# Threshold attention and a SoLU feed-forward: keys turned by VectorE's block transposes instead of TensorE, keys and values loaded in longer runs

## The chip, the cores and the metric

The kernel runs on one core of a Trainium2 chip. Its time is the device time of one execution in microseconds (us); lower is better. The core has five engines that run at once, each through its own list of instructions in order: PE (TensorE, matrix products, with PEld its weight loads), DVE (VectorE), ACT (ScalarE), POOL (GpSimd) and SP (SyncE, which here only issues transfers). Transfers run on 16 DMA engines. SBUF is the memory that all engines work on, PSUM the one that PE writes its products to.

## The reference

There are 8 batches of 8 heads, 576 positions and 64 dimensions, all float32. Per head:

```python
scores = scale * np.matmul(q, k.transpose(0, 1, 3, 2))
thresh = np.max(scores, axis=-1, keepdims=True) - tau
scores = np.where(scores >= thresh, scores, -1000000000.0)
attn = np.exp(scores - np.max(scores, axis=-1, keepdims=True))
attn = attn / (np.sum(attn, axis=-1, keepdims=True) + 1e-09)
out = np.matmul(attn, v)
```

The heads are put side by side (4608 tokens of 512), and each token goes through a feed-forward block: `h = x @ w_in` (1024 wide), `h * softmax(h)`, a layer norm with gain `g_ln`, and `@ w_out`.

## The kernel before, in words

**Pairs and slots.** Two heads make a pair, four pairs (`NP`) a batch, 32 pairs in all; pair i is (b, hp). A pair's q and k are turned so that the 64 dimensions lie on partitions, the first head on rows 0 to 63 and the second on rows 64 to 127 (`ROWS`). A *slot* is a unit of attention, 18 for each batch (`PER`), 144 in all: 128 queries of one pair against its 576 keys (kinds 0 and 1), or, in the last two slots of a batch (kind 2), the 64 last rows ("ends") of two pairs at a time. The main loop (L789) makes one *round* for each slot and hands out each engine's instructions in a fixed, hand-written order. No planner changes it.

**One round.** PE first turns what a later pair needs (`turn`, L281: products with an identity matrix, into the spare columns of the scores' PSUM), then computes the scores (L417). DVE takes the row maximum (L439), ACT the ramp that puts what lies under the threshold out of play (L454) and the exponential (L463), POOL scales by the sum (L473), and DVE turns the weights in blocks of 32 x 32 (L485, tile T). After every second slot SP moves T to wT by four transfers (L496), so that the keys lie on partitions. Three rounds after the slot, PE multiplies wT by v (L521, tile pv). The scores' PSUM has one buffer for each head, so the next scores wait for the ramp and for the copies of turned data (`keep` functions) that were made from it.

**Feed-forward between.** Beside the attention, each round takes half of one of the feed-forward's two products: rounds in which half of the first product runs (h_ps, L577 or L567) are called *hidden rounds* here, those with half of the second (o_ps, L681) *output rounds*. A tile of tokens takes four rounds, in a cycle of two hidden and two output rounds. In the steady stage the products pv are taken in hidden rounds alone. Between the two products lie the softmax and norm (L592 to L648), a swap of parts by four transfers V<-u (L659), and a block transpose (L669, uT).

**Turning q and k.** For pairs from batch 1 on, a list `preps` (L727) says from which round on a pair is turned: k in two items (3 and 1 units), the ends (1 unit) and q (4 units), with room for 7 units in a round. A unit is four calls of `matmul` on 64 x 64 tiles. So k and the ends go in one round and q in the next. What PE has turned is copied out of PSUM, one row half by ACT and the other by DVE: L345 for k, L365 for the ends of k, L361 for the ends of q, L320 and L324 for q. Pairs 0 to 3 are turned through own buffers (tp) at the start.

**Loads.** q and k come four heads at a time (L129), rows 0 to 511 as runs of four positions (1024 bytes), and the 64 end rows in runs of 256 bytes (L140). v comes for four heads in three such parts (L159) and two parts of end rows (L164); both row halves hold all keys in an order of their own (`m ^ 4 * u` in L522). `load_at` (L741) says after which round each load is issued; SP issues them all in order, between the moves of wT, the swaps and the stores of the output.

**Buffers.** `loads` has two buffers for each of q, k and ends and three for v; `heads` has seven for each of qT, kT and qe (a pair's turned q, k and end queries).

Of the kernel before, what the change touches and what calls it, by code (L numbers as in the profile page):

```python
# [8 lines left out]
F32 = mybir.dt.float32  # L9
# [7 lines left out]
P = 128  # L17
# [3 lines left out]
def kernel(  # L21
# [27 lines left out]
    nc = tc.nc  # L49
    B, H, S, D = q.shape  # L50
    DM, DFF = w_in.shape
    SM = 512
    ST = S - SM
    NP = H // 2
    NPAIR = B * NP
    NC = DFF // P
# [3 lines left out]
    ROWS = (slice(0, 64), slice(64, P))  # L60

    const = ctx.enter_context(tc.tile_pool(name="const", bufs=1))
    loads = ctx.enter_context(tc.tile_pool(name="loads", bufs=2))
    heads = ctx.enter_context(tc.tile_pool(name="heads", bufs=7))
    work = ctx.enter_context(tc.tile_pool(name="work", bufs=2))
# [11 lines left out]
    zero = const.tile([P, 1], F32, name="zero")  # L77
    ntau = const.tile([P, 1], F32, name="ntau")
    scl = const.tile([P, 1], F32, name="scl")
    g_rows = const.tile([NC, P], F32, name="g_rows")  # L80
    gs = const.tile([P, NC], F32, name="gs")
    lims = [const.tile([P, 1], F32, name=f"lim{x}") for x in range(2)]

# [5 lines left out]
    NK = S // 64  # L89

    halves = {}
    ends = {}
    pairs = {}
    units = {}
# [25 lines left out]
    def load_one(b, hf, nm, queue=None):  # L120
        d = halves.setdefault((b, hf), {})
        hs = slice(4 * hf, 4 * hf + 4)
        src, rows = {"q": (q, ROWS[0]), "k": (k, ROWS[1])}[nm]
        d[nm] = loads.tile([P, 4, 4, D], F32, tag=nm, name=nm)

        parts = [slice(0, 2), slice(2, 4)] if b == 0 and hf == 0 else [slice(0, 4)]
        for x, part in enumerate(parts):
            queue = nc.scalar if nm == "k" and x + 1 < len(parts) else nc.sync
            queue.dma_start(  # L129
                out=d[nm][:, part].rearrange("p h t d -> p h (t d)"),  # L130
                in_=src[b, hs, 0:SM, :][part].rearrange("h (p t) d -> p h (t d)", t=4),
            )
            if hf == 0 and x == 0:
                if b not in ends:
                    ends[b] = loads.tile([P, H, D], F32, tag="ends", name="ends")
                load_ends(b, nm, slice(0, 2) if len(parts) > 1 else slice(0, H), queue)
# [11 lines left out]
    def load_v(b, hf, parts=(0, 1, 2)):  # L148
        d = halves.setdefault((b, hf), {})
        hs = slice(4 * hf, 4 * hf + 4)  # L150

        if 0 in parts:
            d["v"] = loads.tile([P, 4, NK, D], F32, tag="v", bufs=3, name="v")
        rest = v[b, hs, 0:SM, :].rearrange("h (p t) d -> p h (t d)", t=4)
        for part, to, rows, of in (
            (0, 0, slice(0, P), slice(0, P)), (1, 4, ROWS[0], ROWS[1]), (1, 4, ROWS[1], ROWS[0])
        ):
            if part in parts:
                nc.sync.dma_start(  # L159
                    out=d["v"][rows, :, to : to + 4].rearrange("p h t d -> p h (t d)"),  # L160
                    in_=rest[of],
                )
        for rows in ROWS if 2 in parts else ():
            nc.sync.dma_start(  # L164
                out=d["v"][rows, :, NK - 1], in_=v[b, hs, SM:S, :].rearrange("h p d -> p h d")
            )

    def constants():
# [109 lines left out]

    SPARE = 7

    def turn(spare, x, lhsT_of):  # L281

        o = spare["base"] + 64 * x
        to = slice(o, o + 64)
        for r in range(2):
            for y in range(2):
                nc.tensor.matmul(
                    out=spare[r][ROWS[y], to], lhsT=lhsT_of(r, y), rhs=ident[ROWS[r], ROWS[r]],
                    start=True, stop=True,
                )  # L290
# [9 lines left out]
    def pair(i):  # L300
        if i not in pairs:
            pairs[i] = dict(
                qT=heads.tile([P, SM], F32, tag="qT", name="qT"),
                kT=heads.tile([P, S], F32, tag="kT", name="kT"),
                qe=heads.tile([P, ST], F32, tag="qe", name="qe"),
            )
        return pairs[i]
# [23 lines left out]
    def k_parts(i):  # L331

        return pair(i)["kT"].rearrange("p (c m k) -> p m c k", c=2, m=NK)

    def k_item(i, ts=slice(0, 4)):
        src, h0 = source(i)
        to = k_parts(i)
        n = ts.stop - ts.start

        def make(spare, x):  # L340
            for t in range(n):
                turn(spare, x + t, lambda r, y: src["k"][ROWS[r], h0 + y, ts.start + t])

        def keep(spare, x, r):
            (nc.vector.tensor_copy if r and not spare.get("eased") else nc.scalar.copy)(  # L345
                out=to[:, 4 * r + ts.start : 4 * r + ts.stop],
                in_=seen(spare, r, x, n).rearrange("p t (k c) -> p t c k", c=2),
            )

        return n, make, keep  # L350

    def e_item(i):
        src, h0 = source(i)
        last = k_parts(i)[:, NK - 1]

        def make(spare, x):
            turn(spare, x, lambda r, y: ends[i // NP][ROWS[r], 2 * (i % NP) + y])

        def keep(spare, x, r):
            if r == 0:  # L360
                nc.scalar.activation(  # L361
                    out=pair(i)["qe"], in_=seen(spare, 0, x, 1)[:, 0], func=AF.Copy, scale=scl
                )
            else:
                (nc.scalar.copy if spare.get("eased") else nc.vector.tensor_copy)(  # L365
                    out=last, in_=seen(spare, 1, x, 1)[:, 0].rearrange("p (k c) -> p c k", c=2)
                )

        return 1, make, keep
# [130 lines left out]
    def attend_steps(key):  # L500
        b, kind, hp = key
        unit = units[key]
        wT = unit["wT"]
        unit["y"] = take("pv")
        _, y = unit["y"]
        y = y.rearrange("p (u n) -> p u n", u=2)

        for e in range(2) if kind == 2 else [None]:
            for m in range(NK):
                for u in range(2):  # L510
                    d, h0 = source(b * NP + (hp if e is None else e + 2 * u))
                    for h in range(2):
                        if e is None:
                            to = y[ROWS[h], u, 0:P].rearrange("p (r g x) -> p g r x", r=2, g=2)
                            rhs = wT[ROWS[u], :, m, :, h]
                        else:
                            to = y[ROWS[h], u, 64 * e : 64 * e + 64].rearrange(
                                "p (g x) -> p g x", g=2
                            )
                            rhs = wT[ROWS[u], :, m, e, h]  # L520
                        nc.tensor.matmul(  # L521
                            out=to, lhsT=d["v"][ROWS[u], h0 + h, m ^ 4 * u if m < 8 else m],  # L522
                            rhs=rhs,
                            start=m == 0, stop=m == NK - 1,
                        )
                        yield
# [188 lines left out]
    PER = NS // B  # L715
# [11 lines left out]
    preps = []  # L727
    for i in range(NP, NPAIR):
        b, hp = divmod(i, NP)
        if b == 1:  # L730
            at = (13, 15, 19, 20)[hp]
        else:
            at = PER * (b - 1) + ((6, 12, 16, 21) if b == 2 else (6, 9, 12, 17))[hp]
        preps += [
            (at, 3, lambda i=i: k_item(i, slice(0, 3)), i),
            (at, 1, lambda i=i: k_item(i, slice(3, 4)), i),
            (at, 1, lambda i=i: e_item(i), i),
            (at, 4, lambda i=i: q_item(i), i),
        ]

    load_at = {}  # L741
    for b in range(1, B):
        r = PER * (b - 1)

        for at, job, hf, what in (
            (-1 if b > 1 else 11, load_one, 0, "q"),
            (1 if b > 1 else 9, load_one, 0, "k"),
            (7 if b > 1 else 13, load_one, 1, "k"),
            (9 if b > 1 else 15, load_one, 1, "q"),
            (11 if b > 1 else 17, load_v, 0, (0,)),  # L750
            (13 if b > 1 else 19, load_v, 0, (1, 2)),
            (PER + 3, load_v, 1, (0,)),
            (PER + 5, load_v, 1, (1, 2)),
        ):
            load_at.setdefault(r + at, []).append(
                lambda b=b, job=job, hf=hf, what=what: job(b, hf, what)
            )

    with tc.manual_schedule():
        nc.scalar.dma_start(out=tau_t, in_=tau.partition_broadcast(P))  # L760
# [20 lines left out]
        rnd = 0  # L781
# [7 lines left out]
        while True:  # L789
# [88 lines left out]
            elif step == ("h", 1):  # L878
# [8 lines left out]
                at = rnd + 4 if more or not ready else rnd + 6  # L887
# [9 lines left out]
            elif step == ("o", 1):  # L897
                if prev is not None:
                    ff_o(prev, 1)
                    last = not (more or ready or cur or between)  # L900
# [14 lines left out]
                blocks(rnd - 1)  # L915
            for job in late.pop(rnd, []):
                job()
            if rnd == 3:
                gains()
            if rnd in pieces:  # L920
                x = pieces[rnd]
# [44 lines left out]
```

## Time and profile before

| what | before |
|---|---|
| time, median of 3 runs | 894.29 us (893.82 to 898.87) |
| the profiled execution: time, span | 894.54 us, 892.7 us |
| PE, PEld busy | 848.9 us (95%), 655.3 us (73%) |
| DVE, ACT, POOL busy | 673.8 (75%), 595.6 (67%), 469.3 us (53%) |
| granted PE clock, mean | 0.980 |
| bytes moved by DMA, mean rate | 154.61 MB, 173 GB/s |
| the 288 moves wT<-T: size, time to landing | 288 KB each, median 5.8 us (3.9 to 9.8) |
| loads of k, 512 KB and 1024-byte runs | 6.6 us to landing |
| block transpose L485, 128 x 576 | 288 of 751 ns |
| copies of k out of PSUM (L345, L365): DVE | 352, 216 and 216 ns |
| the same on ACT (L345) | 316 and 224 ns |

A busy share is the time in which an engine had an instruction under way. PE's matmuls overlap, so its share alone does not say that it is at its limit; the distance between the starts of blocks of matmuls does. A float32 matmul call is in the records as two instructions, with two weight loads. A wait is written as "engine line <- engine line": who waited, and whose work ended the wait. Rounds are numbered from 0; round 70 starts at 404.52 us, round 144 would be the first after the attention.

### The profile page before, as it was taken

The numbers are of one execution on the slowest core, as the hardware profiler recorded it, in microseconds if no ns is written. First come the engines' busy times: TensorE is split into PE (matmuls) and PEld (weight loads), VectorE is DVE, ScalarE is ACT, GpSimd is POOL, SyncE is SP. The second block draws the span as 40 slices with busy tenths as digits, with TensorE's granted clock in tenths as the row PEclk, the third lists the DMA queues.
The fourth block names the chain that finished last, engine by engine and source line by source line (L and its number), as shares of the span: only waits on it lengthen the run. The fifth ranks groups of instructions, "written<-read, shape, count | busy, mean of one in ns | idle before, by whom it ended". The sixth has DMA issues, their size and how long they took to land. (4 is left out here: it accounts for less than half of the span.)

```text
span 892.7 us, 39669 instructions
## 1 busy us (share of the span) xinstructions
PE 848.9 (95%) x17089; PEld 655.3 (73%) x17089; DVE 673.8 (75%) x1296; ACT 595.6 (67%) x1249; POOL 469.3 (53%) x888
## 2 busy tenths in 40 slices
PE   5667999999999999999999999999999999999997
PEld 3345677878687877777788887887788777777655
DVE  5989786888777777777777877777777877887451
ACT  5967776777776767777677776677667776676121
POOL 2877655555455555555545555555555555555120
PEclk9868899999999999999999999999999999999999
DMA  7999979796877777777777777877877766766322
GB/s 230 258 251 252 220 184 208 178 219 156 198 173 171 167 179 163 191 172 168 175 182 169 176 168 178 182 174 157 191 184 178 181 132 149 169 139 134 76 48 48
DMA packets 95502, 154.61 MB, mean 173 GB/s; under 512 B 27224, under 2 KB 69216, under 8 KB 95328
## 3 DMA queue, kind: packets, MB, share of 16 engines
q1 hardware_dynamic: 94192, 150.09, 72.5%
q8 instruction: 134, 2.20, 1.1%
q10 hardware_dynamic: 1136, 2.00, 0.7%
q14 instruction: 40, 0.33, 0.1%
HBM read 46.14 MB, written 9.44 MB: 62 GB/s over the span
## 5 line engine op out<-in xcount | busy, mean ns | idle before, releaser
L439 DVE CUSTOM_DVE_ANT_0 w<-s_ps,tau_t 128x576 f32<-128x576 f32 x280 | 200.8, 754 | 145.3 <-PE s_ps L417 123.6
L454 ACT ACTIVATE w<-s_ps,nth 128x576 f32<-128x576 f32 x280 | 201.8, 744 | 109.5 <-DVE nth L439 86.6
L681 PE MATMUL o_ps<-w,uT 64*64 64x256 f32 x4608 | 269.6, 376 | 1.3 <-DVE uT L669 1.0
L681 PEld LDWEIGHTS o_ps<-w,uT 64*64 64x64 f32 x4608 | 235.5, 133 | 42.0 <-ACT xh L544 10.0
L473 POOL TENSOR_SCALAR w<-w,sm 128x576 f32<-128x576 f32 x288 | 217.3, 766 | 14.3
L577 PE MATMUL h_ps<-w,xh 64*64 64x512 f32 x1856 | 224.3, 592 | 0.5 <-issue 0.5
L463 ACT ACTIVATE w<-w,ntau 128x576 f32<-128x576 f32 x288 | 220.4, 772 | 0.0
L485 DVE STREAM_TRANSPOSE T<-w 128x576 f32<-128x576 f32 x288 | 206.0, 751 | 6.5 <-POOL w L473 6.1
L521 PEld LDWEIGHTS pv<-wT,v 64*64 64x64 f32 x5760 | 175.7, 136 | 42.6 <-issue 24.3
L417 PE MATMUL s_ps<-kT,qT 64*64 64x64 f32 (+1 forms) x2048 | 175.6, 424 | 13.7 <-ACT w L454 12.6
L521 PE MATMUL pv<-wT,v 64*64 64x128 f32 (+1 forms) x5760 | 177.2, 263 | 6.3 <-issue 2.2
L577 PEld LDWEIGHTS h_ps<-w,xh 64*64 64x64 f32 x1856 | 116.9, 134 | 79.2 <-issue 56.6
L470 POOL TENSOR_SCALAR sm<-sm 128x2 f32<-128x2 f32 x144 | 36.3, 252 | 247.8 <-ACT w L463 244.7
L471 POOL TENSOR_TENSOR sm<-sm,mone 128x2 f32<-128x2 f32 x144 | 104.7, 727 | 12.0
L417 PEld LDWEIGHTS s_ps<-kT,qT 64*64 64x64 f32 x2048 | 67.9, 139 | 20.0 <-ACT w L454 18.1
L643 ACT ACTIVATE V<-u,nb,rs 128x1024 f32<-128x1024 f32 x36 | 44.7, 1241 | 52.1 <-POOL nb L633 52.1
L544 ACT COPY xh<-pv 128x256 f32<-128x256 f32 x64 | 23.7, 370 | 65.2 <-PE pv L521 65.2
L463 ACT ACTIVATION_READ_ACCUMULATOR w<-w,ntau 128x1 f32 x288 | 56.9, 198 | 0.0
L592 DVE TENSOR_REDUCE hm<-h_ps 128x1 f32<-128x1024 f32 x36 | 43.2, 1200 | 12.6 <-PE h_ps L577 6.3
L607 DVE TENSOR_TENSOR u<-h_ps,u 128x1024 f32<-128x1024 f32 x36 | 42.8, 1190 | 10.3 <-ACT u L601 10.3
L601 ACT ACTIVATE u<-h_ps,hm 128x1024 f32<-128x1024 f32 x36 | 40.3, 1120 | 12.3 <-DVE hm L592 6.8
L669 DVE STREAM_TRANSPOSE uT<-V 128x1024 f32<-128x1024 f32 x36 | 43.9, 1218 | 6.1 <-DMA V<-u 5.8
(81 smaller groups left out, 652.1 us busy)
## 6 DMA issues: line engine op xcount, KB each, us to landing
wT<-T SPq DMA_DIRECT2D x288, 288.0 KB, 5.8
V<-u SPq DMA_DIRECT2D x144, 64.0 KB, 3.5
out_dram<-ob SPq DMA_DIRECT2D x71, 128.0 KB, 2.6
v<-in_v_dram SPq DMA_DIRECT2D x16, 512.0 KB, 6.3
v<-in_v_dram SPq DMA_DIRECT2D x32, 256.0 KB, 6.1
q<-in_q_dram SPq DMA_DIRECT2D x15, 512.0 KB, 6.1
k<-in_k_dram SPq DMA_DIRECT2D x15, 512.0 KB, 6.6
raw<-in_moe_w_out_dram SPq DMA_DIRECT2D x8, 512.0 KB, 8.4
```

What stands on the lines that cost most here:

```text
L417: nc.tensor.matmul(out=ps[h][ROWS[y], ks], lhsT=lhsT, rhs=d["kT"][ROWS[h], ks], start=True, stop=True,)
L439: nc.vector.tensor_tensor_reduce(out=w, in0=ps[:, 0:S], in1=(zero if loose else tau_t).to_broadcast([P, S]), scale=1.0, scalar=BIG, op0=AL ...
L454: nc.scalar.activation(out=d["w"][x], in_=d["w"][x] if d["loose"] else d["ps"][x][:, 0:S], func=AF.Prelu, bias=d["nth"][x], scale=-1.0, al ...
L463: nc.scalar.activation(out=w, in_=w, func=AF.Exp, bias=ntau, scale=1.0, accum_out=sm[:, x : x + 1])
L471: nc.gpsimd.tensor_tensor(out=sm, in0=sm, in1=mone, op=ALU.pow)
L473: nc.gpsimd.tensor_scalar(out=w, in0=w, scalar1=sm[:, x : x + 1], scalar2=1.0, op0=ALU.mult, op1=ALU.mult)
L485: nc.vector.transpose(out=T[:, :, r, h, :], in_=w)
L521: nc.tensor.matmul(out=to, lhsT=d["v"][ROWS[u], h0 + h, m ^ 4 * u if m < 8 else m], rhs=rhs, start=m == 0, stop=m == NK - 1,)
L577: mm = nc.tensor.matmul(out=h[ROWS[y], f], lhsT=x[ROWS[r], c, ROWS[y]], rhs=w1_parts[ROWS[r], c, part ^ r], start=part == 0 and c == 0, st ...
L643: nc.scalar.activation(out=V, in_=u, func=AF.Identity, bias=nb, scale=rs)
L669: nc.vector.transpose(out=uT, in_=d["V"].rearrange("p y (m x) -> p m y x", x=32))
L681: nc.tensor.matmul(out=d["o"][ROWS[z], 512 * r : 512 * r + 256], lhsT=d["uT"][ROWS[r], m].rearrange("p y x -> p (y x)"), rhs=w2[ROWS[r], m ...
```

## The change

From batch 2 on:

- k is no longer turned by PE. `load_natural` loads one pair's k in four transfers of 32 partitions, each partition one run of nine positions (2304 bytes), into a buffer of tag "k". Three rounds later `turn_natural`, called at the end of a round of `turn_at`, lets DVE turn it in blocks of 32 x 32 (source step two floats) into the tile flip, and two transfers of 64 partitions each move flip to kT.
- The k items leave `preps`. The ends item keeps only the end rows of q (`rows=1` in `turn`); k's end rows now come with the rest, and are not loaded by themselves.
- v comes in four transfers for four heads, two heads and one row half each, in runs of 2304 bytes, at other rounds than before; the order of its keys is the plain one, so L522's swap of halves falls away. The order of kT's columns fits it.
- qT has six buffers instead of seven, flip one, and g_rows moves into the buffer of V.

Batches 0 and 1 are loaded and turned as before, and q in all batches.

```diff
-    g_rows = const.tile([NC, P], F32, name="g_rows")
+    g_rows = work.tile([NC, P], F32, tag="V", bufs=1, name="g_rows")
...
     def load_v(b, hf, parts=(0, 1, 2)):
...
+        if b > 1:
+            if 0 in parts:
+                d["v"] = loads.tile([P, 4, NK, D], F32, tag="v", bufs=3, name="v")
+            for part in parts:
+                two, u = divmod(part, 2)
+                nc.sync.dma_start(
+                    out=d["v"][ROWS[u], 2 * two : 2 * two + 2].rearrange("p h m d -> p h (m d)"),
+                    in_=v[b, hs][2 * two : 2 * two + 2].rearrange("h (p m) d -> p h (m d)", m=NK),
+                )
+            return
...
+    def load_natural(i):
+        b, hp = divmod(i, NP)
+        src = k[b, 2 * hp : 2 * hp + 2].rearrange("h (i a t) d -> a h i (t d)", a=2, t=NK)
+        raw = loads.tile([P, 4, 4, D], F32, tag="k", name="k")
+        natural[i] = raw = raw.rearrange("p h t d -> p (h t d)")[:, 0 : NK * D]
+        for g in range(4):
+            a, h = divmod(g, 2)
+            nc.sync.dma_start(out=raw[32 * g : 32 * g + 32], in_=src[a, h])
+
+    def turn_natural(i):
+        raw = natural.pop(i)
+        flip = loads.tile([P, 2, NK, 32], F32, tag="flip", bufs=1, name="flip")
+        nc.vector.transpose(out=flip, in_=raw.rearrange("p (t x g) -> p g t x", g=2, x=32))
+        to = pair(i)["kT"]
+        for a in range(2):
+            nc.sync.dma_start(
+                out=to[:, 32 * NK * a : 32 * NK * (a + 1)],
+                in_=flip[ROWS[a]].rearrange("p g t x -> p g (t x)"),
+            )
...
-    def turn(spare, x, lhsT_of):
+    def turn(spare, x, lhsT_of, rows=2):
...
-        for r in range(2):
+        for r in range(rows):
...
-                qT=heads.tile([P, SM], F32, tag="qT", name="qT"),
+                qT=heads.tile([P, SM], F32, tag="qT", bufs=6, name="qT"),
...
-            turn(spare, x, lambda r, y: ends[i // NP][ROWS[r], 2 * (i % NP) + y])
+            turn(
+                spare, x, lambda r, y: ends[i // NP][ROWS[r], 2 * (i % NP) + y],
+                2 if i < 2 * NP else 1,
+            )
...
-                            out=to, lhsT=d["v"][ROWS[u], h0 + h, m ^ 4 * u if m < 8 else m],
+                            out=to, lhsT=d["v"][ROWS[u], h0 + h, m ^ 4 * u if m < 8 and b < 2 else m],
...
+        if b == 1:
+            preps += [
+                (at, 3, lambda i=i: k_item(i, slice(0, 3)), i),
+                (at, 1, lambda i=i: k_item(i, slice(3, 4)), i),
+            ]
         preps += [
-            (at, 3, lambda i=i: k_item(i, slice(0, 3)), i),
-            (at, 1, lambda i=i: k_item(i, slice(3, 4)), i),
             (at, 1, lambda i=i: e_item(i), i),
             (at, 4, lambda i=i: q_item(i), i),
         ]
...
+    for i in range(2 * NP, NPAIR):
+        b, hp = divmod(i, NP)
+        if b == 2:
+            at = (24, 30, 34, 39)[hp]
+        else:
+            at = PER * b + 4 * hp - (11 if b % 2 else 13)
+        turn_at[at] = i
+        load_at.setdefault(at - 3, []).append(lambda i=i: load_natural(i))
+        if hp % 2:
+            load_at.setdefault(PER * (b - 1) + (9 if hp == 3 else -1), []).append(
+                lambda b=b, hf=hp // 2: load_one(b, hf, "q")
+            )
+            at, by = (PER * b + 4, 1) if hp == 3 else (PER * b - 9, 2)
+            for part in range(4):
+                load_at.setdefault(at + by * part, []).append(
+                    lambda b=b, hf=hp // 2, part=part: load_v(b, hf, (part,))
+                )
...
             for job in late.pop(rnd, []):
                 job()
+            if rnd in turn_at:
+                turn_natural(turn_at[rnd])
```

More of the change, by code (lines that the diff above doesn't have):

```diff
@@ L91 @@
     halves = {}
+    natural = {}
     ends = {}
@@ L353, in e_item @@
         src, h0 = source(i)
-        last = k_parts(i)[:, NK - 1]
+        last = k_parts(i)[:, NK - 1] if i < 2 * NP else None
         def make(spare, x):
-            turn(spare, x, lambda r, y: ends[i // NP][ROWS[r], 2 * (i % NP) + y])
+            turn(
+                spare, x, lambda r, y: ends[i // NP][ROWS[r], 2 * (i % NP) + y],
+                2 if i < 2 * NP else 1,
+            )
         def keep(spare, x, r):
@@ L363, in keep @@
                 )
-            else:
+            elif last is not None:
                 (nc.scalar.copy if spare.get("eased") else nc.vector.tensor_copy)(
@@ L741 @@
     load_at = {}
[L742 to L756, printed above, removed]
-            )
+    turn_at = {}
+    for at, job, hf, what in (
+        (11, load_one, 0, "q"),
+        (9, load_one, 0, "k"),
+        (13, load_one, 1, "k"),
+        (15, load_one, 1, "q"),
+        (17, load_v, 0, (0,)),
+        (19, load_v, 0, (1, 2)),
+        (PER + 3, load_v, 1, (0,)),
+        (PER + 5, load_v, 1, (1, 2)),
+    ):
+        load_at.setdefault(at, []).append(lambda job=job, hf=hf, what=what: job(1, hf, what))
+    for i in range(2 * NP, NPAIR):
[9 more added lines that the diff above has]
+                lambda b=b, hf=hp // 2: load_one(b, hf, "q")
+            )
+            at, by = (PER * b + 4, 1) if hp == 3 else (PER * b - 9, 2)
[3 more added lines that the diff above has]
+                )
     with tc.manual_schedule():
```

## The prediction

> **What bounds the kernel now.** I read the page's busy table first, then TensorE's order of time, then its waits, then the stretches of single rounds, and last the queue of transfers.
>
> ```profile
> PE 848.9 (95%) x17089; PEld 655.3 (73%) x17089; DVE 673.8 (75%) x1296; ACT 595.6 (67%) x1249; POOL 469.3 (53%) x888
> PE   5667999999999999999999999999999999999997
> PEclk9868899999999999999999999999999999999999
> DMA  7999979796877777777777777877877766766322
> ```
>
> Only PE is near its limit, from the sixth slice on (112 us). A busy PE can still be a slow one, so I look at when its blocks start:
>
> ```profile
> 404.52 1.25 PE L417 MATMUL s_ps<-kT,qe 64*64 64x64 f32 x16
> 405.50 3.72 PE L681 MATMUL o_ps<-w,uT 64*64 64x256 f32 x64
> 408.95 0.68 PE L287 MATMUL s_ps<-ident,k 64*64 64x64 f32 x31
> 427.18 1.25 PE L417 MATMUL s_ps<-kT,qT 64*64 64x64 f32 x16
> 428.15 3.72 PE L681 MATMUL o_ps<-w,uT 64*64 64x256 f32 x64
> 431.61 1.24 PE L417 MATMUL s_ps<-kT,qT 64*64 64x64 f32 x16
> 443.47 0.60 PE L521 MATMUL pv<-wT,v 64*64 64x128 f32 x8
> ```
>
> Each block starts where the one before it ends: scores 0.97 us, half of an output product 3.45, scores again. A round with an output half and no turning lasts 431.61 - 427.18 = 4.43 us. The one at 404.52 lasts 5.01, because 40 turning records stand before the next scores at 409.53:
>
> ```profile
> 404.52:409.53 5.01, 5.01 (x124) 4.64 (x120) 4.55 (x10) 3.59 (x8) 3.08 (x7) 1.00 0.43 117
> 427.18:431.61 4.43, 4.43 (x86) 4.06 (x82) 3.96 (x9) 3.03 (x7) 2.66 (x5) 1.00 0.81 186
> 409.53:416.37 6.84, 6.84 (x165) 4.98 (x161) 4.76 (x11) 5.19 (x12) 3.93 (x10) 1.00 0.74 159
> 130.00:820.00 690.00, 685.03 (x14320) 547.91 (x14312) 541.52 (x1050) 485.27 (x1016) 374.27 (x731) 1.00 0.75 173
> ```
>
> Columns: stretch, length, PE, PEld, DVE, ACT, POOL, clock, DMA share. From 130 to 820 us PE idles 5 us in 690, at full clock. So the end is set by PE's work, and work taken off PE shortens the kernel until something else comes late. What could come late:
>
> ```profile
> 417.56 0.76 DVE L439 CUSTOM_DVE_ANT_0 w<-s_ps,tau_t 128x576 f32<-128x576 f32 x1 [2.35 <-PE s_ps L417]
> 432.61 3.52 SPq L496 DMA_DIRECT2D wT<-T x4
> PE s_ps L417 <- ACT w L454: 12.6, 13, 2.8
> ```
>
> First, the softmax loop: scores, maximum, ramp, then the scores buffer is free. In the output rounds its last ramp ends 2.9 us after the scores start, 1.5 us before PE wants the buffer; the waits of PE's scores for the ramp (12.6 us) lie before 130 us. Second, the weights' way T, wT, product: here the four wT transfers are issued from 432.61, the last lands at 442.02, PE reads at 443.47.
>
> [...] a turning record lasts 222 ns, yet 40 of them take 0.58 us, 14.6 ns each. [...] 576 columns 751 ns, 1024 columns 1218, so 1.04 ns a column. [...]
>
> **The change, part by part.**
>
> *PE.* A fp32 matmul leaves two records: k's 16 calls a pair make 896 records on 28 pairs, 32 each. Before, a pair costs k (32 records) and ends (8) in one round, 0.58 us, and q (32) in the next, 6.84 - 6.37 = 0.47 (6.37 being 0.97 + 3.43 + 1.97 for scores, hidden half and product): 1.05. After, q (32) and half of the ends (4) fit one round: 36 x 14.6 = 0.53, or 0.59 if the four, all on one row half, run at half the concurrency. Saved 0.46 to 0.52; I take 0.48. Batches 2 to 7 have 24 pairs: 24 x 0.48 = **11.5 us**. PV and scores keep their number of matmuls.
>
> *VectorE and ScalarE.* Removed per pair: on DVE 352 + 216 + 216 = 784 ns, on ACT 316 + 224 = 540. Added on DVE: one 128x576 transpose, 751 ns by L485[...]. I take 751. In batches 3 to 7 it falls at the end of rounds 43, 47, 51, ..., each the first hidden round of a cycle, after which DVE idles 2.35 us before the next maximum (the line at 417.56), so it costs nothing, even at 1.5 us. Uncovered it would cost 24 x 0.75 = 18 us. If raw is late, DVE stalls with the maximum, the ramp and PE queued behind it: the four loads go out three rounds earlier, at least 4.43 + 4.43 + 6.37 = 15.2 us, against 4 x 0.66 us of issue and 6.6 us (k's own row) of landing. Nothing.
>
> *kT by transfer.* Two moves of 144 KB after the transpose, between 3.5 us (64 KB, V) and 5.8 us (288 KB, wT) to land; the first read is five rounds later or more (turned at the end of round 55, read from slot 60 on: 21.6 us). Nothing.
>
> *SP's queue.* Per batch k has 3 transfers and v 10 before, k 24 (16 loads, 8 moves) and v 8 after: 19 more, 114 in all, at 0.66 us some 75 us of SP, which now waits 190 us for DVE's T. Each of SP's transfers also waits for the one eight before it (the trace shows eight semaphores in turn). What they are moved past: the kT moves stand behind V's swap and the store and before the next wT, which has 5 to 8 us in hand; k's loads stand behind that wT. The tight wT, sent after the second output round, has at most a load of v ahead of it. Taken at nothing; above, 1 us of delay for the roomy ones.
>
> *Bytes.* k's and v's are as before, in longer runs; kT's moves add 48 x 144 KB = 7 MB to 154.6, DMA share 0.75 to 0.78. Not below nothing, since PE waits for no load now.
>
> *Buffers.* qT with six: pair (b, 2) takes the buffer of (b-1, 0), last read three rounds before. g_rows in V's place is read in round 3. Nothing.
>
> *Where the gain is lost.* Batch 2's pairs are prepared in rounds 24 to 39 (146 to 234 us), where some rounds are set by the softmax loop (the one at 176.9 lasts 6.56 us with 4.87 of PE work): up to 1.9 us, I take 0.8. The product of the end rows in batches 3, 5 and 7 (rounds 56, 92, 128) starts 0.52, 0.24 and 0.13 us after its wT landed, and comes 0.5 earlier now: up to 1.4, I take 0.6.
>
> Sum: 11.5 - 0.8 - 0.6 = **10.1 us**. The profiled execution took 894.54 (span 892.7 and 1.8 around it), so 884.4; it lay 0.25 above the median of 894.29, which gives **884.2 us**, 1.1% less.
>
> **Rivals.**
>
> *Transfers eat part (887 to 892).* In cycles without turning the tight product (second hidden round) has 0.9 to 2.1 us in hand after its wT (1.45 at 443.47). If added moves and the eight-deep order delay wT by about 1.7 us, some cycles lose 0.3 us each. For: DMA share 0.75, first issue to last landing swings from 7.2 to 11. Against: moves stand behind that wT in the queue.
>
> *Slower: wT lands late everywhere (905).* One mechanism, one place: this product in the second hidden round of each cycle, some 30 cycles from round 24 on. With about 1.5 us in hand, a wT later by x costs 30 (x - 1.5): from x = 1.85 it eats the whole 10.1, at 2.2 it gives 884.2 + 30 x 0.7 = 905. For: with the DMA engines 90% busy (before 110 us) that time was 10.3 to 12.0 us instead of 8.7. Against: the share rises by three points only.
>
> *Nothing gained (893).* Shorter rounds expose the softmax loop. Against: it has 1.5 us in hand, the change takes 0.5 and also lightens ACT. That the change leaves turning on PE is a case of this; the diff leaves q and the end rows of q.
>
> **Chances.** Forecast 0.67, transfers eat part 0.18, nothing gained 0.06, slower 0.09. A measurement of this kernel tells about 1% from no change, the bound here 885.35 and 903.2. The forecast's own spread (0.46 to 0.52 a pair, the two losses) is 881.5 to 886.5, six in seven of it beyond 1%: faster 0.57; same 0.10 + 0.18 + 0.06 = 0.34; slower 0.09. Range 881.5 to 890: nearly all of the forecast, over half of the second case.
>
> **What would show it.** Right: the k group of L287 falls from 896 records to 128; rounds with an output half keep 4.43 us, or 4.43 + 0.55 with turning; the new transpose lasts 0.75 us and shortens the idle time before the next maximum to 1.6; PE idle stays below 1% from 130 us on. Wrong: PE's products waiting for wT, DVE's new transpose waiting for raw, or PE's scores waiting for kT's moves.

## The result, and the profile after

| what | before | after |
|---|---|---|
| time, median of 6 runs each | 895.04 us (893.82 to 899.77) | 885.72 us (882.72 to 888.09) |
| ratio, with its 95% interval | | 0.988 (0.9848 to 0.9913) |
| the profiled execution: time, span | 894.54, 892.7 us | 883.54, 881.8 us |
| PE, PEld busy | 848.9, 655.3 us | 835.4, 592.1 us |
| DVE, ACT busy | 673.8, 595.6 us | 682.0, 586.3 us |
| bytes moved | 154.61 MB | 161.60 MB |

The kernel became 1.2% faster; 884.2 us, 1.1% less, was forecast. The first lines of the page of after, in the order in which those of before were read (busy time, PE's slices, granted clock, share of the DMA engines):

```profile
PE 835.4 (95%) x16225; PEld 592.1 (67%) x16225; DVE 682.0 (77%) x1248; ACT 586.3 (66%) x1201; POOL 471.0 (53%) x888
...
PE   5667999989999999999999999999999999999997
...
PEclk9878899999999999999999999999999999999999
DMA  7999978887878796988789787888779777866222
```

PE keeps its 95%, of a shorter span: it is still the engine that the end waits for. The same output rounds as before, in order of time:

```profile
399.75 1.20 PE L451 MATMUL s_ps<-kT,qe 64*64 64x64 f32 x16
400.73 3.67 PE L715 MATMUL o_ps<-w,uT 64*64 64x256 f32 x64
...
404.35 0.63 PE L318 MATMUL s_ps<-ident,q 64*64 64x64 f32 x29
...
421.94 1.20 PE L451 MATMUL s_ps<-kT,qT 64*64 64x64 f32 x16
...
426.37 1.19 PE L451 MATMUL s_ps<-kT,qT 64*64 64x64 f32 x16
```

Where k stood (ident,k), q stands now (ident,q). The round without turning lasts 426.37 - 421.94 = 4.43 us as before. Stretches (columns as in the prediction), the first being the output round with turning, the second the hidden round that follows it, where q was turned before and nothing is turned now:

```profile
399.75:404.76 5.01, 5.01 (x121) 4.06 (x114) 4.54 (x10) 3.73 (x9) 3.02 (x7) 1.00 0.87 203
404.76:411.14 6.38, 6.38 (x134) 4.02 (x130) 5.46 (x10) 5.10 (x11) 3.53 (x9) 1.00 0.77 170
130.00:820.00 690.00, 682.26 (x13600) 489.45 (x13593) 555.62 (x1007) 479.08 (x974) 378.23 (x735) 1.00 0.81 186
```

The first keeps 5.01 us, the second falls from 6.84 to 6.38. That 0.46 us is the gain of a changed pair. From 130 to 820 us PE now idles 7.7 us, 1.1%, in place of 5.0. The k group of turning (count, shortest, median and longest in ns, first and last start):

```profile
L318 PE MATMUL s_ps<-ident,k x128: 216/218/311, 83.1 to 127.2; 64*64 64x64 f32 x128
```

It holds batch 1 alone, and ends at 127 us. The new transpose among the groups by shape (count, busy us, mean ns, idle time before it):

```profile
L191 DVE STREAM_TRANSPOSE flip<-k 128x576 f32<-128x576 f32 x24 | 17.6, 732 | 0.0
```

And one of DVE's waits between 130 and 820 us, before and then after (total us, times, longest):

```profile
DVE uT L669 <- DMA V<-u: 1.4, 4, 0.5
```

```profile
DVE uT L703 <- DMA V<-u: 19.4, 20, 1.8
```

The wait of uT's transpose for the swap V<-u has grown from 1.4 to 19.4 us. It costs DVE idle time, not PE's: none of PE's 7.7 us in that stretch is a wait for uT. It fits a fuller SP queue: SP's transfer records fill 69% of rounds 43 to 133 before and 81% of them now. This comes back below.

To see where the time went I cut the attention by rounds (starts of rounds in the trace; rounds 43 to 133 are the steady part, with 20 of the 24 changed pairs; up to 20 before and after have the same order of work). A second execution of the changed kernel (885.47 us) stands beside the first, the expectation written ahead of it being

> A second look at the changed kernel. Rounds 30 and 31 last 1 us and more longer than in the kernel before again if loads ahead of V's swap are a property of the kernel; round 43 starts between 247 and 252, with waits put to issue of under 1.5 us between 124 and 250 us.

```
                  start of 20   20 to 43   43 to 133   133 to the end
before                124.4       125.7       513.4       129.2
after                 122.5       125.1       504.5       129.6
after, second         124.3       122.3       507.3       129.9
```

The steady part gained about 9 us in one execution and 6 in the other. Up to round 43 the same code varies by several us: round 20 starts between 122.5 and 128.2 us in the profiles of this study. The suspicion about rounds 30 and 31 was not confirmed: they last 7.19 and 8.65 us in the first execution, but 5.60 and 6.95 in the second, against 6.56 and 6.38 before. Round 43 starts at 246.6 us, just below what was expected.

### The profile page after: what moved, and what is told of

It is laid out like the page before. It is cut to its first block, busy times and chain, and to the rows that moved or that the text cites. A ratio compares the mean times of both kernels' runs of the same rounds, so it can differ in the third digit from the quotient of the medians.

```text
span 881.8 us, 38016 instructions
## 1 busy us (share of the span) xinstructions
PE 835.4 (95%) x16225; PEld 592.1 (67%) x16225; DVE 682.0 (77%) x1248; ACT 586.3 (66%) x1201; POOL 471.0 (53%) x888
## 2 busy tenths in 40 slices
DMA packets 85033, 161.60 MB, mean 183 GB/s; under 512 B 19832, under 2 KB 49536, under 8 KB 84864
## 3 DMA queue, kind: packets, MB, share of 16 engines
q8 instruction: 127, 2.08, 1.1%
## 5 line engine op out<-in xcount | busy, mean ns | idle before, releaser
L715 PE MATMUL o_ps<-w,uT 64*64 64x256 f32 x4608 | 265.2, 376 | 1.1 <-DVE uT L703 1.1
L488 ACT ACTIVATE w<-s_ps,nth 128x576 f32<-128x576 f32 x280 | 199.8, 743 | 97.0 <-DVE nth L473 93.1
L715 PEld LDWEIGHTS o_ps<-w,uT 64*64 64x64 f32 x4608 | 218.9, 133 | 58.3 <-issue 13.8
L611 PE MATMUL h_ps<-w,xh 64*64 64x512 f32 x1856 | 220.0, 596 | 0.0
L555 PEld LDWEIGHTS pv<-wT,v 64*64 64x64 f32 x5760 | 166.5, 136 | 51.1 <-issue 36.3
L451 PE MATMUL s_ps<-kT,qT 64*64 64x64 f32 (+1 forms) x2048 | 168.1, 422 | 16.4 <-ACT w L488 12.5
L555 PE MATMUL pv<-wT,v 64*64 64x128 f32 (+1 forms) x5760 | 170.9, 263 | 7.9 <-DMA wT<-T 3.7
L611 PEld LDWEIGHTS h_ps<-w,xh 64*64 64x64 f32 x1856 | 98.3, 135 | 96.6 <-issue 88.6
L451 PEld LDWEIGHTS s_ps<-kT,qT 64*64 64x64 f32 x2048 | 61.8, 139 | 25.1 <-ACT w L488 17.7
L682 DVE TENSOR_SCALAR u<-u,rs,nb 128x1024 f32<-128x1024 f32 x36 | 42.4, 1178 | 12.7 <-ACT V L677 12.4
```

Source lines behind the costliest of these rows:

```text
L451: nc.tensor.matmul(out=ps[h][ROWS[y], ks], lhsT=lhsT, rhs=d["kT"][ROWS[h], ks], start=True, stop=True,)
L488: nc.scalar.activation(out=d["w"][x], in_=d["w"][x] if d["loose"] else d["ps"][x][:, 0:S], func=AF.Prelu, bias=d["nth"][x], scale=-1.0, al ...
L555: nc.tensor.matmul(out=to, lhsT=d["v"][ROWS[u], h0 + h, m ^ 4 * u if m < 8 and b < 2 else m], rhs=rhs, start=m == 0, stop=m == NK - 1,)
L611: mm = nc.tensor.matmul(out=h[ROWS[y], f], lhsT=x[ROWS[r], c, ROWS[y]], rhs=w1_parts[ROWS[r], c, part ^ r], start=part == 0 and c == 0, st ...
L715: nc.tensor.matmul(out=d["o"][ROWS[z], 512 * r : 512 * r + 256], lhsT=d["uT"][ROWS[r], m].rearrange("p y x -> p (y x)"), rhs=w2[ROWS[r], m ...
```

## The experiments

**TensorE's share: the work put back (pe_back).** As after, with 32 turning records a pair of q's data put back on PE from batch 2 on, into spare columns that nobody reads.

```diff
+    def idle_item(i):
+        ...
+            for t in range(4):
+                turn(spare, x + t, lambda r, y: src["q"][ROWS[r], h0 + y, t])
...
+        if b > 1:
+            preps.append((at, 4, lambda i=i: idle_item(i), i))
```

> The changed kernel, with as many turning matmuls put back on PE as k's were (32 records a pair, of q's data, into the spare columns, copied nowhere and used by nothing). The theory of the prediction, that the gain is PE's work: 24 x 0.46 us come back, less what batch 2 hides, so 895 to 897 us, no faster than before. Rival, the gain came from fewer copies or better transfers: at most 888 us, since these stay as in the changed kernel.

Measured: 900.74 us (897.93 to 903.07), ratio to before 1.0059 (1.0037 to 1.008). Rounds 43 to 133 take 514.0 us, 9.5 more than in after's first execution and 6.7 more than in its second; over 20 pairs the 9.5 are 0.48 a pair. Two turning blocks stand in the rounds again, in order of time:

```profile
415.23 0.68 PE L318 MATMUL s_ps<-ident,q 64*64 64x64 f32 x31
...
422.07 0.68 PE L318 MATMUL s_ps<-ident,q 64*64 64x64 f32 x32
```

The second is the hidden round's extra part. Rounds 70 and 71 together last 11.80 us, against 11.39 in after and 11.85 before. With the loads, DVE's transposes and the moves all kept, the steady part is back at before's 513.4. So PE's turning work accounts for the gain of that part, as closely as single executions can tell; fewer copies or better transfers do not. The expectation of 895 to 897 us was missed, however: the kernel ended 5 us above before, because rounds 20 to 43 took 134.3 us, 9.2 more than in after. Four pairs' turning is 1.9 us of this by the prediction's price, and waits of PE put to issue (the profile names nothing that PE waited for) are 4.0, none of 0.4 us or more in after; these waits come back at the end. The rest is not settled.

**k without v, v without k (k_only, v_only).** The first is after with v loaded as before; the second is before with v's new loads alone. In both the weights meet v in another order of keys than the reference's, with the same number and shape of operations.

```diff
# k_only, against after
-        if b > 1:
-            ...  # v in four transfers of 2304-byte runs
-            return
# v_only, against before
+        if b > 1:
+            ...  # v in four transfers of 2304-byte runs
+            return
```

> k as in the changed kernel, v loaded as before in 1024-byte and 256-byte runs at the old rounds (the weights then meet v in another order, so the values are not the attention's; the work is the same). PE theory: as the changed kernel, 884 to 887.5 us. Rival, v's long runs carry part of the gain: 889 to 893 us.

> The kernel before with v alone in 2304-byte runs at the new rounds, k turned by PE (the weights meet v in another order; same work). PE theory: as before, 893.5 to 896.5 us. Rival, v's runs carry part of the gain: 889 to 892 us.

Measured: k_only 884.45 us (883.37 to 887.66), ratio 0.9891 (0.9847 to 0.9935), steady part 503.8; v_only 897.21 us (891.23 to 902.51), ratio 1.0014 (0.9991 to 1.0038), steady part 514.8. The first lies in its expected band, the second 0.7 us above it. As far as the intervals tell, the whole gain goes with k; v's longer runs carry nothing that can be told from no change.

**The change from the fourth batch on (batch3_on).** Batch 2 loaded and turned as before, its PE work 4 x 0.48 = 1.9 us more than after's.

```diff
-        if b == 1:
+        if b < 3:
             preps += [
...
-    for i in range(2 * NP, NPAIR):
+    for i in range(3 * NP, NPAIR):
```

> The whole change, but from the fourth batch on; batch 2 as in the kernel before. The prediction's step (batch 2 gives 1.1 us of the sum): 886 to 887.5 us. Rival from the trace after (rounds 30 and 31 lose 2.9 us there, so batch 2 gives about nothing): 884 to 886 us, and rounds 29 to 31 without the long stalls.

Measured: 892.13 us (886.4 to 896.13, 20 runs), ratio 0.996 (0.9941 to 0.9979): 6.4 us above after, more than either expectation had said. A second execution was profiled:

> A second look at the change from the fourth batch on. If its 6.4 us over the changed kernel belong to turning work of the third batch that TensorE does while its instructions come late behind data (the waits put to issue, each ending 1.2 to 1.7 us after a 16 KB packet of the instruction queue), such waits of 3 us or more stand between 124 and 250 us again and round 43 starts at 253 to 256. If they were one execution's, the waits are under 2 us and round 43 starts by 252.

```
                  start of 20   20 to 43   43 to 133   133 to the end
batch3_on             127.3       128.0       504.8       131.5
batch3_on, second     124.5       123.5       506.3       133.4
```

The steady part is after's. In the second execution (889.63 us) round 43 starts at 248.1, and no wait of PE put to issue of 0.4 us or more stands between 124 and 250 us, so the 7.6 us by which the first was behind at round 43 do not belong to every execution. The second is among the faster ones, though: 18 of the 20 runs took longer, so which of the two is usual is not known. What both share is the end: 1.9 and 3.8 us more than after from round 133 on. The last product o_ps waits for uT there (waits of PE after 800 us, of the second execution and then of after):

```profile
PE o_ps L715 <- DVE uT L703: 2.7, 1, 2.7
```

```profile
PE o_ps L715 <- DVE uT L703: 1.1, 1, 1.1
```

The first execution has the same 2.7, so this accounts for 1.6 us in both. With the 1.9 us of PE work, if it counts in full, it makes 3.5 of the 6.4; the rest is not settled.

**DVE's cover (flip_twice).** Each pair's transpose is made twice, 732 ns more.

```diff
-        nc.vector.transpose(out=flip, in_=raw.rearrange("p (t x g) -> p g t x", g=2, x=32))
+        for _ in range(2):
+            nc.vector.transpose(out=flip, in_=raw.rearrange("p (t x g) -> p g t x", g=2, x=32))
```

> The changed kernel with each new block transpose of k made twice into the same tile (24 more of 0.73 us on DVE). The prediction's step (covered by DVE's idle time before the next maximum): rounds 43 to 133 stay at 504.5 us within 0.7, and that idle time falls by another 0.7 us at the turning rounds. Rival, DVE is close enough to the path that its work counts: up to 20 x 0.73 = 15 us longer.

Measured, one run: 886.83 us, within after's 882.72 to 888.09; steady part 505.5, between after's two, though 0.3 us beyond the band that was expected. The idle time that covers the transpose, 1.21 us in after, falls by 0.81:

```profile
414.20 0.76 DVE L474 CUSTOM_DVE_ANT_0 w<-s_ps,tau_t 128x576 f32<-128x576 f32 x1 [0.40 <-PE s_ps L452]
```

The new transpose is hidden, and even two of them, 1.46 us a pair, leave some idle time.

**The ends on both row halves (ends_both).** As after, but the ends item makes eight records again instead of four, the other four of data that nobody reads.

```diff
-                2 if i < 2 * NP else 1,
...
+                lambda r, y: ends[i // NP][ROWS[r], 2 * (i % NP) + y]
+                if r == 0 or i < 2 * NP else src["q"][ROWS[r], h0 + y, 0],
```

> The changed kernel, with the ends item on both row halves of PE again (the second half turns q's data for nothing; copied nowhere). If the four records on one row half run at half the concurrency, as the 5.01 us of the turning rounds suggests, the four on the other half are free: turning rounds stay at 5.01 us and rounds 43 to 133 at 504.5 within 0.5. If a record costs 14.6 ns whatever its place: 5.07 and 505.7.

Measured, one run: 894.32 us, steady part 510.2. The turning rounds themselves last 5.01 us, as with four records (rounds 66, 70, 90, 102, 126 in both). So leaving k's half of the ends out saved PE nothing in these rounds: 40 records on both row halves and 36 with four on one half take the same time. The steady part missed its expectation by far, and the run lies 6 us above the slowest of after. The 5.7 us of the steady part lie elsewhere, 2.3 and 2.9 of them in rounds 56 and 92, the products of the end rows; round 92 was 2.1 longer in after's second execution too. From one run it stays open whether they are the edit's.

**wT later (wt_late).** The four moves to wT after the second output round go as eight of half the size from round 26 on.

```diff
-                nc.sync.dma_start(out=to[ROWS[half], g], in_=T[of : of + 32])
+                if s < 24 or s % 4 != 1:
+                    nc.sync.dma_start(out=to[ROWS[half], g], in_=T[of : of + 32])
+                    continue
+                for j in range(2):
+                    a = 64 * half + 32 * j
+                    nc.sync.dma_start(
+                        out=to[a : a + 32, g], in_=T[of + 16 * j : of + 16 * j + 16]
+                    )
```

> The changed kernel, with the wT moves after the second output round of each cycle in eight transfers of half the size, from round 26 on: SP needs 4 x 0.66 = 2.6 us longer to issue them, the bytes are the same. The rival that was forecast slower (wT lands late for the product of the second hidden round, 0.1 to 4.3 us in hand by the trace after): with a delay of 2.0 to 2.6 us, rounds 43 to 133 last 11 to 19 us longer, in waits of the product for wT. If this product had more in hand than the trace says: under 3 us.

Measured: 903.98 us (899.63 to 906.4), ratio to before 1.0075 (1.0045 to 1.0105); steady part 517.5, 13.0 above after, as expected, 8.8 of it in second hidden rounds. PE's waits for wT between 124 and 820 us, where after has 1.4:

```profile
PE pv L562 <- DMA wT<-T: 7.0, 8, 1.8
```

The slower rival's mechanism exists, at its place, and the margin is about as small as it said: four more small moves a cycle turn the gain into a loss. The waits for wT are 7.0 of the 18.3 us by which the kernel is slower than after; the rest is not traced to its causes, and 4.9 us of it in the profiled execution come after round 133.

**Batch 2's loads spread (b2_loads).** Pair 9's k is loaded two rounds earlier, the first half of v later, so that they do not stand ahead of V's swap before round 31.

```diff
-        load_at.setdefault(at - 3, []).append(lambda i=i: load_natural(i))
+        load_at.setdefault(25 if i == 9 else at - 3, []).append(lambda i=i: load_natural(i))
...
-            at, by = (PER * b + 4, 1) if hp == 3 else (PER * b - 9, 2)
+            at, by = (PER * b + 4, 1) if hp == 3 else (PER * b - 9 + 4 * (b == 2), 2 - (b == 2))
```

> The changed kernel, with pair 9's k loaded after round 25 instead of 27 and the first half of v of batch 2 after rounds 31 to 34 instead of 27 to 33, so that only q is loaded after round 27, ahead of V's swap. If these loads made the swap and uT late and so the long rounds 30 and 31 (7.19 and 8.65 us): both 1 to 2 us shorter, time 883 to 885.5 us. If those rounds are long for another reason: no change, 885 to 887 us.

Measured: 884.35 us (882.97 to 887.81), ratio 0.9854 (0.9826 to 0.9883) beside after's 0.988 (0.9848 to 0.9913): no difference shown. Rounds 30 and 31 last 5.30 and 6.95 us, but the second execution of after has them at 5.60 and 6.95 without the edit. The long rounds that suggested it were one execution's.

**The same for q (q_too).** If PE's turning is the price, q's should be worth as much again. From batch 2 on q is loaded in 2048-byte runs, scaled by ACT, turned by DVE behind k's transpose and moved by two transfers of 64 partitions; PE keeps the end queries.

```diff
+    def turn_q(i):
+        raw = halves[i // NP, i % NP // 2]["q"][:, i % 2]
+        flip = work.tile([P, DM], F32, tag="ob", name="flipq")
+        nc.vector.transpose(
+            out=flip.rearrange("p (g z x u) -> p g u z x", g=2, z=4, u=2),
+            in_=raw.rearrange("p (u z x g) -> p g u z x", g=2, z=4, u=2),
+        )
+        to = pair(i)["qT"]
+        for a in range(2):
+            nc.sync.dma_start(
+                out=to[:, 256 * a : 256 * a + 256],
+                in_=flip[ROWS[a]].rearrange("p (g n) -> p g n", g=2),
+            )
...
-            (at, 4, lambda i=i: q_item(i), i),
+        if b == 1:
+            preps.append((at, 4, lambda i=i: q_item(i), i))
```

> The change carried on to q: from the third batch q too is loaded in 2048-byte runs, scaled by ScalarE, turned by VectorE and moved by two 64-partition transfers of 128 KB; only the end queries (4 records a pair) stay on TensorE. If TensorE's work sets the end: 32 records fewer on 24 pairs, 24 x 0.47 = 11.3 us, and about 6 of the 16 KB packets of PE's instructions fewer: 885.7 - 11 gives 873 to 877, rounds 43 to 133 take 495 to 496 us in place of 504.5, rounds with turning 4.5 instead of 5.0. If the margin of wT and uT is used up (132 more transfers on SP's queue, VectorE 0.7 us more a pair), it stays at 880 to 890, with waits of pv for wT and of uT for V over 5 us more than after's.

> The kernel with q moved as well, and with batch 2's loads spread (pair 9's k two rounds earlier, the first half of v later): if rounds 30 and 31 still wait for V behind loads, 1 to 3 us below the kernel with q moved alone, 872 to 875; if moving q has already changed that order, the same within 1 us.

Measured: 899.34 us (896.69 to 901.99), ratio to before 1.0034 (1.0009 to 1.0059), and with batch 2's loads spread (q_and_b2) 899.24 us (893.57 to 906.14, 19 of 20 runs; one took 908.92), ratio 1.0041 (1.0017 to 1.0064). Slower than before, not faster than after, and slower than even the second expectation, 880 to 890. The turning rounds fell from 5.01 to 4.54 us as forecast, yet the steady part takes 520.3 us, 15.9 more than after; second hidden rounds alone took 21.1 more. The stretch from 270 to 765 us, first of after, then of this kernel:

```profile
270.00:765.00 495.00, 492.09 (x9857) 355.89 (x9851) 401.27 (x726) 345.97 (x702) 272.97 (x535) 1.00 0.82 188
```

```profile
270.00:765.00 495.00, 476.67 (x9016) 337.78 (x9012) 393.58 (x703) 338.36 (x683) 270.58 (x519) 0.99 0.84 193
```

PE idles 18.3 us there in place of 2.9. Its waits for wT in that stretch, and DVE's for V:

```profile
DVE uT L735 <- DMA V<-u: 38.6, 19, 3.7
...
PE pv L587 <- DMA wT<-T: 13.7, 15, 2.9
```

(after has 13.2 and 0.2 us.) The profiled execution of q_and_b2, with 893.97 us one of the fastest of its kind, shows the same thing smaller: a steady part of 511.9 us, 14.5 us more than after in second hidden rounds, waits of 36.2 and 10.0. Why wT lands late is seen in one cycle in order of time, with SP's transfers, DVE's turning of T and PE's product:

```profile
492.13 5.08 SPq L562 DMA_DIRECT2D wT<-T  x4
497.25 4.92 SPq L186 DMA_DIRECT2D k<-in_k_dram  x4
498.42 1.38 DVE L551 STREAM_TRANSPOSE T<-w 128x576 f32<-128x576 f32 x2
502.22 0.62 SPq L158 DMA_DIRECT2D v<-in_v_dram  x1
502.95 3.78 SPq L562 DMA_DIRECT2D wT<-T  x4
...
511.11 0.44 PE L587 MATMUL pv<-wT,v 64*64 64x128 f32 x4 [1.10 <-DMA wT<-T]
```

T was complete at 499.80, but SP was issuing loads until 502.84 and sent the first move 3.15 us late. In after SP was through with the loads by 492.68, T was complete at 494.94, and the same move left at once:

```profile
492.04 0.64 SPq L158 DMA_DIRECT2D v<-in_v_dram  x1
495.00 4.25 SPq L530 DMA_DIRECT2D wT<-T  x4
```

Over the 23 second hidden rounds of the steady part, the means from the trace (T complete to the first move issued, first to fourth move issued, fourth issued to the last landed, and the slack from landing to PE's product; in us). The last two columns take only the rounds for which the trace has the fourth move's landing, 19, 11, 19 and 19 of them, so the rows do not compare quite the same rounds:

```
                T to first move   first to fourth   fourth to landed   slack
before               0.06              2.88              5.82           1.82
after                0.07              2.79              5.87           0.99
after, second        0.14              2.88              6.03           1.06
q_too                1.27              2.75              6.08           0.59
```

In q_too the moves themselves are hardly slower (0.2 us); they start late. T itself is complete 0.90 us after the start of the round before the product, 0.61 in after, so DVE's added transposes are the smaller part. The changed kernel seems to have used some of the slack already. From 492.13 to 506.73 us SP's entries follow each other within 0.11 us, and they fill 87% of q_too's steady part; the DMA engines were busy to 8 tenths in the page's slices from 472 to 517 us. That the time of issue is the cause is read from the traces: issuing part of the transfers from another engine was not tried. Of the versions that ran and compute the attention, after and the one with spread loads are the fastest.

## Why the prediction was right, point by point

**PE's term.** Taken: 24 x 0.48 = 11.5 us, with 0.46 to 0.52 as bounds. Shown by the rounds: 0.46 us a pair, the low bound; the work put back gives 0.48 from one execution. The four remaining records of the ends cost as much as eight did (the prediction's "or 0.59", an estimate; measured 0.58). q_too agrees that four on one row half cost about twice as much each: alone they make its turning rounds 4.54 us instead of 4.43, 28 ns each against 14.6. Behind a product, in round 71 of pe_back, 36 records with four of the ends took only 0.53, so the price depends on what stands beside them. By 0.46 the term was 24 x 0.02 = 0.5 us too large. Its main signs came: 128 records of k, 4.43 us, and 5.01 for 4.98.

**The total.** The mechanism was right, and the sum came within 1.5 us of the median. That closeness is in part luck: the two losses that it takes off, 0.8 and 0.6 us, are not confirmed below, and two executions of the changed kernel differ by more than both in single stages.

**Batch 2.** Taken: 0.8 us lost of 1.9. Rounds 20 to 43 gained 0.6 us in one execution and 3.4 in the other, so the loss is smaller than the difference between two executions there; it can't be judged. That undoing batch 2's part cost 6.4 us was not foreseen.

**The product of the end rows.** Taken: 0.6 us lost in rounds 56, 92 and 128. In the first execution they became 0.23, 0.24 and 0.35 us shorter; in the second 0.66 and 0.38 shorter, and 92 longer by 1.87. The place is where executions differ, but the price was argued from one wT landing and does not hold for both.

**VectorE.** Taken at nothing, right: doubled, it still costs nothing that shows. The idle time before the maximum of that kind of round fell further than forecast, to 1.21 us instead of 1.6. The prediction took off the transpose alone; the hidden round is also 0.46 us shorter, and 2.35 - 0.73 - 0.46 = 1.16 (DVE's copy of q only takes the place that k's copies had in that round):

```profile
412.38 0.76 DVE L473 CUSTOM_DVE_ANT_0 w<-s_ps,tau_t 128x576 f32<-128x576 f32 x1 [1.21 <-PE s_ps L451]
```

**SP's queue and the bytes.** Taken at nothing for the tight wT and up to 1 us of delay for the roomy ones. Measured in the steady part, from T to the first move: tight 0.06 us before and 0.07 after (0.14 in the second execution), roomy 0.48 before and 1.60 after (1.97), a little more than the bound. The price of 0.66 us for an issue was near the median, 0.65 in before and 0.62 in after; the mean in the steady part is 0.90 before and 0.84 after. The order eight deep holds in both traces: of the 574 transfers of before and 483 of after for which the landing of the one eight places ahead is recorded, none starts before that landing, and the nearest starts 0.02 us after it. The 7 MB came as forecast; the DMA share went to 0.81, not 0.78.

**Transfers eat part.** A trace of it came: between 124 and 820 us PE's products wait for wT 1.4 us in after and 2.9 in its second execution, three waits in each, and none that the view lists before. PE's idle time of 1.1% also lies above the 1% that was named as a sign.

**The slower rival.** It did not happen, and its premise is now shown twice: eight moves for four, or q's transfers ahead in the queue, and PE waits in the second hidden rounds. Its figure of about 1.5 us in hand is near the mean slack of before, 1.8; after has about 1.0. (The 10.3 to 12.0 us that it read before 110 us hold for the moves from 34 to 92 us; those at 24.6 and 105.6 us took 8.3 and 8.4.) What it had from the wrong side is the cause: it argued from the share of the DMA engines, and what moved the landing in these two kernels is the time of issue.

## What to carry to other kernels

Where one engine is busy all the time, price a moved step by the distance between the starts of its blocks, and test it by putting the work back. Then count what the step costs in the queue that feeds the next-tightest wait: here k could leave TensorE because SP still issued the tight move at once, and q could not, because loads came to stand ahead of it, for 3 us in the cycle shown and 1.3 on the mean. A profile of one execution shows a mechanism, but not a difference of a few us in a stage that varies by that much.

## What was not expected

**Instructions that come late.** PE has waits of 0.4 to 2.6 us, put to issue, as here in the first execution of the change from the fourth batch on:

```profile
236.99 1.88 PE L611 MATMUL h_ps<-w,xh 64*64 64x512 f32 x13
241.48 2.36 PE L611 MATMUL h_ps<-w,xh 64*64 64x512 f32 x18 [2.61 <-issue]
```

The trace has a queue of its own for instructions, in packets of 16 KB (queue, packets, MB, share; before and then after):

```profile
q8 instruction: 134, 2.20, 1.1%
```

```profile
q8 instruction: 127, 2.08, 1.1%
```

The queue's bytes go with PE's records: 2.20 MB over the 2 x 17089 of before, 2.08 over the 2 x 16225 of after and 1.98 (121 packets) over the 2 x 15457 of q_too all make 64 bytes a record. That it carries PE's instructions is an estimate from these. The packets come all through the execution, in after from 14.4 to 870.5 us. In the 14 profiles of this study there are 43 such waits of PE, of 0.4 us or more, between 100 and 870 us, and in each of them PE goes on 1.1 to 1.7 us after the end of such a packet (at 241.48, 1.5 us after one that ran from 239.03 to 239.96). Packets come some 6.5 us apart, so chance would put about one in eleven there. That PE waits for instructions is what this points to; why a packet starts late, with other transfers on the same engines or otherwise, was not varied on its own.

**Smaller ones.** The block transpose with a source step of two floats takes 732 ns for 576 columns, no more than the plain one, whose 751 was taken for it as an estimate (the 1218 for 1024 columns in the prediction is uT's). The moves of 144 KB to kT land in 2.7 us, under the bounds of 3.5 to 5.8 that were taken for them.
